# An attention with two gated layers in one kernel: first chunk's output products planned among the attention's steps, output copies of the first group on ScalarE, a longer warm-up and a later load

## The chip, the cores and the metric

The kernel runs on one core of a Trainium2 chip. The metric is the time of one execution on the device, in microseconds (us); lower is better. The core's engines are TensorE (PE, with its weight loads PEld), VectorE (DVE), ScalarE (ACT), GpSimd (POOL) and SyncE (SP), which here only issues DMA transfers. Each engine works through its own instructions in the order in which they stand, and waits on semaphores for the others.

## The reference, cut to what matters

```python
batch, n_heads, seq, head_dim = (4, 8, 576, 64)            # attention
scores = scale * np.matmul(q, k.transpose(0, 1, 3, 2))
thresh = np.max(scores, axis=-1, keepdims=True) - tau
scores = np.where(scores >= thresh, scores, -1000000000.0)
attn = softmax(scores);  x = attn @ v                       # x: 2304 tokens x 512
rms = np.sqrt(np.mean(x * x, axis=-1, keepdims=True) + 1e-06)
xn = x / rms * rms_g                                        # layer 1, d_ff = 1536
silu = g * (1.0 / (1.0 + np.exp(-g)))                       # g = xn @ w_gate
x = silu * (xn @ w_val) @ w_out
h = x @ w_in;  out = (h * np.cos(h)) @ w_out2               # layer 2, d_ff = 2048
```

The inputs are float32, except that the five large weights come as 64-bit floats; the kernel turns them into float32 itself.

## The kernel before, in words

**Attention.** The 32 heads are worked in 16 pairs. For a pair the kernel loads q, k and v, and PE transposes k and q in three preparations: `psb` (three quarters of k and its rest), `psa` (q) and `psc` (the last of k and the rests); ScalarE copies each out of PSUM. The rows of a pair form five units. `s_mm` makes the scores of a unit (a score block, tile `s`, two PSUM banks for each of the two heads, single buffered), VectorE copies them out and takes the row maximum (`s_max`), ScalarE makes the exponentials (`e`, for the fifth unit `el`), VectorE masks them and sums rows (`s_mask`), PE transposes the result (`pst`; the parts left over go to a `psc` of their own), ScalarE copies it (`et`), and PE multiplies with v (`po`, twice a pair). ScalarE copies that to `t`, GpSimd divides by the row sums (`xb<-t,rb`), squares it (`sq<-xb`) and adds the squares of a batch (`sq<-sq`); PE sums them over the features (`pss`), and VectorE, GpSimd and a trip through DRAM make the RMS factors `rs`. The attention's output goes to DRAM as well, and comes back in six chunks of 384 tokens.

**Layer 1.** Each chunk is scaled (`scale_x`, GpSimd, tile `acc<-acc,rs`; for the early chunks `xe<-xe`) and split into a high and a low part (`xh` on ScalarE, `xl` on VectorE), since every product is made of three matmuls (`mm3`: high x high, low x high, high x low). Layer 1 runs in six groups of two blocks of 128 features. For every group, chunk and block (numbered by `seq`), `gv_mm` makes the gate and value products (`pgv`, 24 matmuls of 384 columns), then come silu (`hh`), the product, and the split into `hhi` and `hlo`, and `o1` makes the output products (`px`, 12 matmuls into four PSUM banks: one tagged `v`, three tagged `t`, the same banks that the attention uses for `po`, for the transposes and for `pss`). After the second block of a group the four banks are added to `acc[c]`; in the first group (g == 0) they are copied. In the loop `o1` runs one step behind `gv_mm`. The next groups' weights are loaded (`raw`), converted (`wtmp`, with a step on GpSimd) and split (`whi`, `wlo`) on the way.

**Layer 2** follows in the same manner; the change doesn't touch it.

**What sets the order.** The attention and the first four steps of layer 1 (`N_EARLY = 4`: 96 matmuls `pgv` for chunks 0 and 1, without their output products) are steps of a planner, class `Plan`. Each step has an engine, a duration and a place from the table `STEPS`. `order` takes again and again the step that can start first by its own reckoning, and among equals the one with the lowest place, where place = the kind's number in `STEPS` + 3500 for each unit. It knows buffers (`take` and `free`), a port that VectorE and GpSimd share (`LOCK`, `BEHIND`: some GpSimd steps are made to wait for a VectorE instruction), and the PE's cost of changing between kinds of blocks. What it decides is the order of the program; on the chip each engine waits for its data. Ahead of the plan stand by hand: the loads of the first pair, `warm(8)` (products of ones that only keep PE at work), the three preparations of pair 0, with `warm(2)` behind the first. The plan starts with the loads of pair 1. Behind the plan, the rest of layer 1 is a loop written out in code.

Of the kernel before, what the change touches and what calls it, by code (L numbers as in the profile page):

```python
# [9 lines left out]
F32 = mybir.dt.float32  # L10
# [4 lines left out]
ALU = mybir.AluOpType  # L15
# [13 lines left out]
    "none": ("", 0, 27559),  # L29
    "load_k": ("SP", 1700, -172962, 5000),  # L30
    "load_q": ("SP", 1700, -46102, 7000),
    "load_v": ("SP", 1700, -4761, 5000),
    "pb": ("PE", 440, -19143),
    "pa": ("PE", 440, -15661),
    "pc": ("PE", 330, -8379),
    "pb_a": ("ACT", 590, 81106),
    "pa_a": ("ACT", 690, -473960),
    "pc_a": ("ACT", 480, 49428),
    "s": ("PE", 960, -21325),
    "s4": ("PE", 490, 85459),  # L40
    "warm": ("PE", 640, 37404),
    "max": ("DVE", 833, -172383),
    "exp": ("ACT", 785, 72251),
    "th": ("POOL", 300, -18608),
    "mask": ("DVE", 890, -37373),
    "t": ("PE", 438, 31564),
    "raw": ("ACT", 595, -92045),
    "c0": ("PE", 220, -3639),
    "c1": ("PE", 440, -315186),
    "c_raw": ("ACT", 415, 218185),  # L50
    "radd": ("POOL", 250, 94231),
    "rinv": ("DVE", 430, -4519),
    "r_out": ("SP", 2100, -108544, 2500),
    "r_in": ("SP", 1700, -320774, 11000),
    "av0": ("PE", 2110, -371909),
    "av1": ("PE", 2660, -60188),
    "avo": ("ACT", 420, 4517),
    "div": ("POOL", 1410, 8372),
    "xout": ("SP", 500, -179658, 2500),
    "sq": ("POOL", 1145, 63241),  # L60
    "x_add": ("POOL", 1410, 86580),
    "xsum": ("PE", 1150, 399585),
    "mean": ("DVE", 150, -681609),
    "rms": ("POOL", 1520, 138440),
    "rs_out": ("SP", 2500, -32428, 2500),
    "x_load": ("SP", 500, 48239, 6000),
    "x_p": ("POOL", 1010, 169405),
    "x_a": ("ACT", 610, -116593),
    "x_d": ("DVE", 550, 94630),
    "jdma": ("SP", 500, 52341, 5000),  # L70
    "j1": ("DVE", 600, -115045),
    "j2": ("DVE", 690, -98093),
    "j_p": ("POOL", 1310, 466908),
    "j_a": ("ACT", 620, 67088),
    "gv": ("PE", 2100, 18969),
    "silu": ("ACT", 500, -124840),
    "hmul": ("DVE", 560, -259566),
    "hhi": ("ACT", 520, -319947),
    "hlo": ("DVE", 560, -244125),
# [9 lines left out]
WARM = (8, 2, 0, 0)  # L89
# [7 lines left out]
N_EARLY = 4  # L97


class Plan:  # L100
# [19 lines left out]
    def order(self):  # L120
# [16 lines left out]
        while len(out) < len(steps):  # L137
            best = None
            for eng, ns in here.items():
                for n in list(ns):  # L140
                    s = steps[n]
                    held = [taken[tag][-self.bufs[tag]] for tag, _ in s["take"]
                            if len(taken[tag]) >= self.bufs[tag]]
# [46 lines left out]
    def run(self, tc):  # L190


        done = tc.nc.cur_bb.bb.instructions
        wait = mybir.DependencyInfo(mybir.DependencyClass.Sync, mybir.DependencyReason.DATA)
        for s in self.order():
            n = len(done)
            s["fn"]()
            if s["eng"] == "DVE" and s["kind"] in LOCK:
                s["ins"] = done[-1]
            if s.get("behind"):  # L200
                for x in done[n:]:
                    tc.add_manual_dep(x, s["behind"]["ins"].name, wait, reason="port")
# [3 lines left out]
def attention_moe_cos_kernel(  # L206
# [585 lines left out]

    def attention():
# [179 lines left out]
        def grow_2():  # L973
            att_s.close()
            late[2] = ctx.enter_context(tc.tile_pool(name="xhl2", bufs=1, side="right"))
            late["acc", 3] = ctx.enter_context(tc.tile_pool(name="acc3", bufs=1, side="right"))
# [25 lines left out]
        for n in range(N_EARLY):  # L1002
# [8 lines left out]
            hs.append(add("hlo", NU + n, h_lo, n, after=[x], free=[("hh", n)]))  # L1011
        plan.run(tc)

    with tc.manual_schedule():
# [11 lines left out]
        acc_p = ctx.enter_context(tc.tile_pool(name="acc", bufs=NCH - 1))  # L1026
# [3 lines left out]
        late.update({("acc", c): acc_p for c in range(NCH) if c != 3})  # L1030
# [7 lines left out]


        xacc = {}  # L1040

        def o1(n):
            g, c, i = seq[n]
            fs = groups[g][1]
            if i == fs[0]:
                xacc[c] = [
                    (ps_t if d else ps_v).tile(
                        [P, 512], F32, tag="t" if d else "v", name=f"px{d}"
                    )[:, 0:TC]
                    for d in range(KD)  # L1050
                ]
            whi, wlo = slots["1", 2, i]
            h = hq.pop(n)
            for d in range(KD):
                mm3(xacc[c][d], (whi[:, d], wlo[:, d]), h, i == fs[0], i == fs[-1])
            if i == fs[-1]:
                if c not in acc:
                    acc[c] = acc_tile(c, [P, KD, TC])
                for d in range(KD):
                    dst = acc[c][:, d]  # L1060
# [4 lines left out]
                del xacc[c]  # L1065
# [194 lines left out]
```

## Time and profile before

| | before |
|---|---|
| median of 3 runs | 1190.27 us (1190.05 to 1190.27) |
| the profiled execution | 1190.16 us |
| its span, first to last instruction | 1188.4 us |
| PE busy | 1162.2 us, 98% of the span |
| VectorE busy | 798.9 us, 67% |
| ScalarE busy | 647.4 us, 54% |
| GpSimd busy | 313.8 us, 26% |
| chain of work that ended last | PE 91% of the span |

The profile is of one execution. Its page gives the busy time of each engine, the chain of work that ended last, and the costliest groups of instructions; the trace behind it can be asked for stretches of time, for waits and for single instructions. A PE that is busy is not always PE at its peak: matmuls are pipelined, two are under way at a time, and the granted clock can fall to half. So for PE the distance between the starts of two instructions says more than the duration of one.

### The profile page before, as it was taken

What the parts mean: (1) busy time and instruction counts of PE and PEld (TensorE: products, weight loads), DVE (VectorE), ACT (ScalarE), POOL (GpSimd) and SP (SyncE); (2) the same over time, 40 slices, a digit from 0 to 9 for tenths busy, and PEclk for the clock granted to TensorE, in tenths of its full rate; (3) what the DMA queues carried; (4) which work ended last, traced back from release to release, by engine and by line L of the source; (5) the groups of instructions that cost most, each with busy time, mean ns of one, the idle gap of its engine ahead of it and who ended that gap; (6) DMA issues with size and microseconds to landing.
All of it is one profiled execution on the core that took longest, in us unless ns stands there. A gap on an engine that the chain in (4) does not pass through costs nothing.

```text
span 1188.4 us, 18206 instructions
## 1 busy us (share of the span) xinstructions
PE 1162.2 (98%) x6832; PEld 1021.9 (86%) x6832; DVE 798.9 (67%) x1571; ACT 647.4 (54%) x1210; POOL 313.8 (26%) x299
## 2 busy tenths in 40 slices
PE   8999999999989999999999999999999999999997
PEld 6666666666779999999999999999999999999996
DVE  5787787877547572642735538579688696876765
ACT  5887877777424231321312214377676676766663
POOL 1223435423543120110201102014334243332222
PEclk9999999999989999999999999999999999999999
DMA  5434424112352130110300202102112021000014
GB/s 130 111 95 126 105 75 131 51 41 71 121 165 72 54 107 1 46 61 1 91 17 23 85 1 59 49 1 71 36 37 71 1 71 36 18 19 1 1 53 107
DMA packets 99448, 71.66 MB, mean 60 GB/s; under 512 B 65040, under 2 KB 89360, under 8 KB 99360
## 3 DMA queue, kind: packets, MB, share of 16 engines
q1 hardware_dynamic: 98256, 70.20, 21.0%
q8 instruction: 54, 0.88, 0.3%
q10 hardware_dynamic: 1040, 0.26, 0.1%
q14 instruction: 34, 0.28, 0.1%
q0 software_dynamic: 64, 0.03, 0.0%
HBM read 60.95 MB, written 9.52 MB: 59 GB/s over the span
## 4 chain that ended last, share of the span: by engine, by line
PE 91%; issue 3%; DVE 2%; ACT 1%; POOL 1%; DMA 1%; SPq 0%; POOLq 0%; DVEq 0%; ACTq 0%
PE pgv L736 23%; PE ph L736 16%; PE po L736 16%; PE px L736 11%; PE s L504 8%; PE po L630 7%; PE pst L593 5%; PE psc L612 1%; PE psa L438 1%; PE warm L702 0%; PE psb L438 0%; DMA raw<-in_moe_w_out_dram 0%; DVE wtmp L308 0%; DVE hlo L772 0%; ACT et L603 0%
## 5 line engine op out<-in xcount | busy, mean ns | idle before, releaser
L736 PE MATMUL pgv<-xl,whi 128*128 128x384 f32 x576 | 193.9, 337 | 0.0
L736 PE MATMUL pgv<-xh,whi 128*128 128x384 f32 x576 | 193.9, 337 | 0.0
L736 PE MATMUL pgv<-xh,wlo 128*128 128x384 f32 x576 | 193.7, 336 | 0.0
L312 POOL TENSOR_TENSOR wtmp<-wtmp,raw 128x512 int32<-128x512 int32 x68 | 93.5, 1375 | 364.4 <-DVE wtmp L308 347.7
L1165 POOL TENSOR_TENSOR hlo<-r,hhi 128x384 fp32r<-128x384 f32 x96 | 98.0, 1021 | 303.7 <-ACT hhi L1164 247.7
L760 ACT ACTIVATE hh<-pgv 128x384 f32<-128x384 f32 x72 | 35.4, 491 | 255.9 <-PE pgv L736 255.9
L764 DVE TENSOR_TENSOR hh<-hh,pgv 128x384 f32<-128x384 f32 x72 | 39.8, 552 | 167.0 <-ACT hh L760 166.9
L736 PE MATMUL ph<-xh,whi 128*128 128x384 f32 x384 | 129.7, 338 | 0.0
L736 PE MATMUL ph<-xl,whi 128*128 128x384 f32 x384 | 129.6, 338 | 0.0
L736 PE MATMUL ph<-xh,wlo 128*128 128x384 f32 x384 | 129.3, 337 | 0.0
L524 DVE TENSOR_SCALAR_CACHE_REDUCE s<-s 128x576 f32<-128x576 f32 x128 | 91.9, 754 | 47.3 <-PE s L504 47.1
L1147 ACT ACTIVATE t<-ph,magic 128x384 f32<-128x384 f32 x96 | 55.8, 581 | 111.4 <-PE ph L736 111.4
L736 PE MATMUL po<-whi,hlo 128*128 128x512 f32 x288 | 114.7, 398 | 1.4 <-POOL hlo L1165 1.4
L736 PE MATMUL po<-whi,hhi 128*128 128x512 f32 x288 | 113.9, 395 | 0.2 <-ACT hhi L1164 0.2
L736 PE MATMUL po<-wlo,hhi 128*128 128x512 f32 x288 | 113.5, 394 | 0.0
L736 PEld LDWEIGHTS pgv<-xl,whi 128*128 128x128 f32 x576 | 108.2, 188 | 0.4 <-DVE xl L730 0.3
L736 PEld LDWEIGHTS pgv<-xh,whi 128*128 128x128 f32 x576 | 108.3, 188 | 0.0
L736 PEld LDWEIGHTS pgv<-xh,wlo 128*128 128x128 f32 x576 | 108.2, 188 | 0.0
L553 DVE SCALAR_TENSOR_TENSOR e<-s,th,e 128x576 f32<-128x576 f32 x128 | 103.1, 840 | 0.5 <-POOL th L534 0.5
L736 PE MATMUL px<-hhi,whi 128*128 128x384 f32 x288 | 98.9, 343 | 3.6 <-DVE acc L1062 3.3
L1154 DVE SCALAR_TENSOR_TENSOR r<-t,r 128x384 f32<-128x384 f32 x96 | 99.4, 1035 | 3.3
L543 ACT ACTIVATE e<-s,m 128x576 f32<-128x576 f32 x128 | 95.7, 783 | 8.2 <-DVE s L524 7.9
(118 smaller groups left out, 2457.6 us busy)
## 6 DMA issues: line engine op xcount, KB each, us to landing
raw<-in_moe_w_out_dram SPq DMA_DIRECT2D x28, 512.0 KB
raw<-in_moe_w_in_dram SPq DMA_DIRECT2D x16, 512.0 KB
raw<-in_moe_w_gate_dram SPq DMA_DIRECT2D x12, 512.0 KB
raw<-in_moe_w_val_dram SPq DMA_DIRECT2D x12, 512.0 KB
x<-xb SPq DMA_DIRECT2D x16, 288.0 KB
kn<-in_k_dram SPq DMA_DIRECT2D x16, 256.0 KB
vn<-in_v_dram SPq DMA_DIRECT2D x16, 256.0 KB
qn<-in_q_dram SPq DMA_DIRECT2D x15, 256.0 KB
```

Of the source, the lines that this page charges most:

```text
L312: nc.gpsimd.tensor_tensor(tmp, tmp, lw, op=ALU.add)
L504: nc.tensor.matmul(ps[:, c, 0:288], lhs, kh[r, k0:k0 + 288], start=True, stop=True,)
L524: nc.vector.tensor_scalar(s.rearrange("p (c n) -> p c n", c=2), un[n].pop(("ps", hd))[:, :, 0:288], qscale[:, 0:1] if n % 5 == 4 else 1.0, ...
L543: nc.scalar.activation(un[n]["e"][:, hd], un[n]["s", hd], AF.Exp, bias=grp[group_of(n)]["m"][:, c], scale=-1.0)
L553: nc.vector.scalar_tensor_tensor(e, un[n].pop(("s", hd)), grp[group_of(n)]["th"][:, ci:ci + 1], e, op0=ALU.is_le, op1=ALU.mult, accum_out= ...
L593: nc.tensor.transpose(ps[:, c], e[:, hd, k0:k0 + P], ident)
L630: nc.tensor.matmul(po[64 * hd:64 * hd + 64, :], vn[:, c, hd, :] if c < 4 else vl[:, hd, :], hf[j]["et"][:, hd, c, :] if c < 4 else hf[j][" ...
L736: nc.tensor.matmul(ps, w[a], x[bb], start=first and i == 0, stop=last and i == 2)
L764: nc.vector.tensor_tensor(hq[n], hq[n], pgv.pop(n)[:, 1, 0:TC], op=ALU.mult)
L1147: nc.scalar.activation(t, ph, AF.Identity, bias=magic[:, 0:1], scale=INV2PI)
L1154: nc.vector.scalar_tensor_tensor(r, t, -C2, r, op0=ALU.mult, op1=ALU.add)
L1165: nc.gpsimd.tensor_tensor(lo, r, f(hi), op=ALU.subtract)
```

## The change

Five things are changed. The warm-up ahead of the keys has 12 products instead of 8, and the 2 behind the first preparation are gone. The load of the second pair's keys waits for the last transpose of the first preparation (`load_k1`, a dependency added by hand). Two steps of output products (`px`, `N_PX = 2`, both blocks of chunk 0, 24 matmuls) and their four copies (`pxc`) are made steps of the plan, so the loop behind it starts with two of them done. The first group's copies of output products go from VectorE to ScalarE. And all numbers of the table `STEPS` that set the places are others, so that the planner's order changes everywhere. Chunk 0's sum moves to the pool of chunk 3's. The rest of the diff moves `o1` to another place in the file and counts two takes of one tag in a step properly.

```diff
 STEPS = {
...
-    "max": ("DVE", 833, -172383),
-    "exp": ("ACT", 785, 72251),
+    "max": ("DVE", 833, -2165065),
+    "exp": ("ACT", 785, 18525),
...
+    "px": ("PE", 2100, 184028),
+    "pxc": ("ACT", 500, 1363803),
...
-WARM = (8, 2, 0, 0)
+WARM = (12, 0, 0, 0)
...
+N_PX = 2
...
+    def px_out(g, c, d):
+        dst = acc[c][:, d]
+        if g == 0:
+            nc.scalar.copy(dst, xacc[c][d])
+        else:
+            nc.vector.tensor_tensor(dst, dst, xacc[c][d], op=ALU.add)
...
         for kind, m in zip("bac", WARM[1:]):
             prep_pe(0, kind)
+            if kind == "b":
+                first = tc.nc.cur_bb.bb.instructions[-1]
             prep_act(0, kind)
             warm(m)
+        def load_k1(p):
+            done_ = tc.nc.cur_bb.bb.instructions
+            n = len(done_)
+            load_k(p)
+            for x in done_[n:]:
+                tc.add_manual_dep(x, first.name, SYNC, reason="first loads")
...
-                lk[p] = add("load_k", n, load_k, p, take=[("kn", ("kn", p))])
+                lk[p] = add("load_k", n, load_k if p > 1 else load_k1, p, take=[("kn", ("kn", p))])
...
+        y = add("none", 999, lambda: acc.__setitem__(0, acc_tile(0, [P, KD, TC])), after=[g2])
+        z = None
+        for n in range(N_PX):
+            z = add("px", NU + n + 3, px_mm, n, after=[hs[n], z],
+                take=[] if n else [("v", ("px", 0))] + [("t", ("px", d)) for d in range(1, KD)],
+            )
+        for d in range(KD):
+            add("pxc", NU + 5, px_out, 0, 0, d, after=[z, y], free=[("v" if not d else "t", ("px", d))] if 0 else [("px", d)])
...
-                    if g == 0:
-                        nc.vector.tensor_copy(dst, xacc[c][d])
-                    else:
-                        nc.vector.tensor_tensor(dst, dst, xacc[c][d], op=ALU.add)
...
-        done = 0
+        done = N_PX
```

PE, early in the attention, where the second pair's scores meet the first's last transposes (`s_500` and `s_529` are the scores of two units, `el` the fifth unit's, `psa` the queries' preparation). Before:

```order
L617 MATMUL psc<-ident,el 64x128
L593 MATMUL pst<-ident,e 128x128 x8
L504 MATMUL s_500<-k,q 128x288
L504 MATMUL s_501<-k,q 128x288
...
L504 MATMUL s_529<-k,q 128x288
L504 MATMUL s_530<-k,q 128x288
...
L438 MATMUL psa<-ident,qn 128x128 x4
```

Now, at the same unit:

```order
L449 MATMUL psb<-ident,k_424 128x128
L444 MATMUL psb<-ident,kn 128x128 x3
L510 MATMUL s_531<-k,q 128x288
L510 MATMUL s_532<-k,q 128x288
...
L636 MATMUL po<-et,vn 64x320 x8
L636 MATMUL po<-ec,v_95 64x320 x2
L510 MATMUL s_568<-k,q 128x288
L510 MATMUL s_569<-k,q 128x288
```

The two score blocks that stood one behind the other have the first pair's second value products between them.

PE, at the end of the attention: the fifth unit's transposes of the last pair, its second value products `po`, the early gate and value products `pgv` (96), the last batch's row sums `pss` and the first output products `px`. Before:

```order
L593 MATMUL pst<-ident,el 128x128 x4
L736 MATMUL pgv<-xh,whi 128x384
...
L736 MATMUL pgv<-xh,wlo 128x384
L630 MATMUL po<-et,vn 64x320 x8
L630 MATMUL po<-ec,v_96 64x320 x2
L670 MATMUL pss<-ones,sq 128x1 x5
L736 MATMUL px_4139<-hhi,whi 128x384
```

Now:

```order
L599 MATMUL pst<-ident,el 128x128 x4
L636 MATMUL po<-et,vn 64x320 x8
L636 MATMUL po<-ec,v_96 64x320 x2
L742 MATMUL pgv<-xh,whi 128x384
...
L742 MATMUL px_4078<-hhi,wlo 128x384
L676 MATMUL pss<-ones,sq 128x1 x5
L742 MATMUL px_4174<-hhi,whi 128x384
```

The last value products have moved ahead of the 96, and the 24 output products of chunk 0 stand between the 96 and the row sums.

GpSimd, from the scaling of chunk 2 on (`xe`): the last batch's power (`r_149`), the scaling of chunks 3, 4 and 5 (`acc<-acc,rs`) and the weights' additions (`wtmp`). Before:

```order
L723 TENSOR_TENSOR xe<-xe 128x384 x2
L681 TENSOR_TENSOR r_149<-r_149,expo 128x5
L789 TENSOR_TENSOR acc<-acc,rs 128x1536
L312 TENSOR_TENSOR wtmp<-wtmp,raw 128x512 x3
L789 TENSOR_TENSOR acc<-acc,rs 128x1536
L312 TENSOR_TENSOR wtmp<-wtmp,raw 128x512 x2
```

Now:

```order
L729 TENSOR_TENSOR xe<-xe 128x384 x4
L795 TENSOR_TENSOR acc<-acc,rs 128x1536
L687 TENSOR_TENSOR r_149<-r_149,expo 128x5
L318 TENSOR_TENSOR wtmp<-wtmp,raw 128x512
L795 TENSOR_TENSOR acc<-acc,rs 128x1536
L318 TENSOR_TENSOR wtmp<-wtmp,raw 128x512 x2
```

The power and the scaling of chunk 3 have changed places, and one weight addition instead of three stands ahead of the scaling of chunk 4.

## Rows read from the trace of the kernel before

**Rows 1.** Stretch, its length; busy us of PE, PEld, DVE, ACT, POOL; clock; DMA, GB/s

```profile
10.00:305.00 295.00, 288.35 (x2163) 193.88 (x2164) 234.19 (x634) 226.78 (x412) 100.07 (x114) 1.00 0.36 94
...
328.00:335.00 7.00, 5.21 (x20) 5.21 (x21) 1.43 (x4) 1.23 (x2) 6.20 (x6) 0.51 0.07 25
335.00:400.00 65.00, 61.38 (x347) 59.76 (x346) 43.49 (x73) 22.82 (x44) 22.09 (x12) 1.00 0.42 128
400.00:1100.00 700.00, 699.58 (x3766) 668.29 (x3765) 449.02 (x734) 334.21 (x638) 147.39 (x127) 1.00 0.13 38
```

**Rows 2.** What PE waited for: us in total, times, longest

```profile
PE s L504 <- DVE s L524: 5.2, 7, 0.9
PE pss L670 <- POOL sq L661: 4.9, 1, 4.9
PE px L736 <- DVE acc L1062: 3.3, 3, 1.7
PE psb L443 <- DMA k<-in_k_dram: 2.4, 1, 2.4
...
PE pst L593 <- ACT et L603: 0.7, 1, 0.7
```

**Rows 3.** Instructions in order of time, start: start us, us, operation, [idle before]

```profile
7.34 1.06 PE L702 MATMUL warm<-ones 128*128 128x128 f32 x4
7.59 0.58 ACT L472 COPY k<-psb 128x512 f32<-128x512 f32 x1 [4.83 <-PE psb L438]
...
8.20 1.06 PE L438 MATMUL psa<-ident,qn 128*128 128x128 f32 x4
...
9.30 0.69 ACT L470 ACTIVATE q<-psa,qscale 128x512 f32<-128x512 f32 x1 [1.12 <-PE psa L438]
```

**Rows 4.** The same view of PE, second of two score blocks in a row

```profile
35.76 1.43 PE L504 MATMUL s<-k,q 64*128 64x288 f32 x6 [0.85 <-DVE s L524]
```

**Rows 5.** The same view: earlier row sums, then the attention's end on four engines

```profile
144.50 1.17 PE L670 MATMUL pss<-ones,sq 128*128 128x1 f32 x10
...
301.55 1.70 DVE L553 SCALAR_TENSOR_TENSOR el<-s,th,el 128x576 f32<-128x576 f32 x1 [0.21 <-POOL th L534]
...
305.00 0.42 PE L736 MATMUL pgv<-xh,whi 128*128 128x384 f32 x1
305.28 0.59 ACT L603 COPY et<-pst 128x512 f32<-128x512 f32 x1
...
325.44 1.40 POOL L647 TENSOR_TENSOR xb<-t,rb 128x576 f32<-128x576 f32 x1 [1.83 <-ACT t L640]
...
329.79 2.29 PE L670 MATMUL pss<-ones,sq 128*128 128x1 f32 x10 [4.89 <-POOL sq L661]
331.94 0.67 PE L736 MATMUL px<-hhi,whi 128*128 128x384 f32 x1
...
335.52 0.34 PE L736 MATMUL pgv<-xh,whi 128*128 128x384 f32 x1
...
339.68 0.34 PE L736 MATMUL px<-hhi,whi 128*128 128x384 f32 x1
```

**Rows 6.** PE's waits for the copies, and two groups of copies (count, busy, mean ns)

```profile
342.68 0.44 PE L736 MATMUL px<-hhi,whi 128*128 128x384 f32 x1 [0.75 <-DVE acc L1062]
...
353.00 0.41 PE L736 MATMUL px<-hhi,whi 128*128 128x384 f32 x1 [1.73 <-DVE acc L1062]
...
L1062 DVE COPY acc<-px 128x384 f32<-128x384 f32 x24 | 11.7, 547 | 0.0
...
L472 ACT COPY k<-psc 128x384 f32<-128x384 f32 x16 | 7.6, 474 | 0.9 <-PE psc L458 0.9
```

**Rows 7.** GpSimd's scaling of chunk 4, and PE's first products of chunk 4

```profile
356.56 3.50 POOL L789 TENSOR_TENSOR acc<-acc,rs 128x1536 f32<-128x1536 f32 x1
...
367.73 0.34 PE L736 MATMUL pgv<-xh,whi 128*128 128x384 f32 x1
```

More of the change, by code (lines that the diff above doesn't have):

```diff
@@ L28 @@
 STEPS = {
[L29 to L41, printed above, removed]
-    "max": ("DVE", 833, -172383),
-    "exp": ("ACT", 785, 72251),
@@ L44 @@
[L44 to L79, printed above, removed]
+    "none": ("", 0, 989236),
+    "load_k": ("SP", 1700, -2080791, 5000),
+    "load_q": ("SP", 1700, -71929, 7000),
+    "load_v": ("SP", 1700, 1092105, 5000),
+    "pb": ("PE", 440, -510840),
+    "pa": ("PE", 440, -238233),
+    "pc": ("PE", 330, 5527),
@@ new lines @@
+    "pb_a": ("ACT", 590, -16795),
+    "pa_a": ("ACT", 690, -1741191),
+    "pc_a": ("ACT", 480, -1089184),
+    "s": ("PE", 960, -2067487),
+    "s4": ("PE", 490, -536410),
+    "warm": ("PE", 640, -512436),
+    "max": ("DVE", 833, -2165065),
+    "exp": ("ACT", 785, 18525),
+    "th": ("POOL", 300, -79889),
+    "mask": ("DVE", 890, -806542),
+    "t": ("PE", 438, 45402),
+    "raw": ("ACT", 595, -536576),
+    "c0": ("PE", 220, -1677441),
+    "c1": ("PE", 440, -448255),
+    "c_raw": ("ACT", 415, -134803),
@@ L80 @@
+    "hmul": ("DVE", 560, 68682),
+    "hhi": ("ACT", 520, -551420),
+    "hlo": ("DVE", 560, -825852),
 }
@@ L141, in order @@
                     s = steps[n]
-                    held = [taken[tag][-self.bufs[tag]] for tag, _ in s["take"]
-                            if len(taken[tag]) >= self.bufs[tag]]
+                    tags = [tag for tag, _ in s["take"]]
+                    at = [(tag, len(taken[tag]) + tags[:i].count(tag) - self.bufs[tag]) for i, tag in enumerate(tags)]
+                    held = [taken[tag][i] for tag, i in at if i >= 0]
                     wait = [key for key in held if users.get(key, 1)]
@@ L201, in run @@
                 for x in done[n:]:
-                    tc.add_manual_dep(x, s["behind"]["ins"].name, wait, reason="port")
+                    tc.add_manual_dep(x, s["behind"]["ins"].name, SYNC, reason="port")
 @with_exitstack
@@ L791, in scale_x, with px_open, px_mm, o1 @@
         )
+    xacc = {}
+    def px_open(c):
+        xacc[c] = [
+            (ps_t if d else ps_v).tile([P, 512], F32, tag="t" if d else "v", name=f"px{d}")[:, 0:TC]
+            for d in range(KD)
+        ]
+    def px_mm(n):
+        g, c, i = seq[n]
+        fs = groups[g][1]
+        if i == fs[0]:
+            px_open(c)
+        whi, wlo = slots["1", 2, i]
+        h = hq.pop(n)
+        for d in range(KD):
+            mm3(xacc[c][d], (whi[:, d], wlo[:, d]), h, i == fs[0], i == fs[-1])
+    def px_out(g, c, d):
[4 more added lines that the diff above has]
+            nc.vector.tensor_tensor(dst, dst, xacc[c][d], op=ALU.add)
+    def o1(n):
+        g, c, i = seq[n]
+        px_mm(n)
+        if i == groups[g][1][-1]:
+            if c not in acc:
+                acc[c] = acc_tile(c, [P, KD, TC])
+            for d in range(KD):
+                px_out(g, c, d)
+            del xacc[c]
     def attention():
@@ L1029, in attention_moe_cos_kernel @@
         late.update({c: x_p for c in range(3, NCH)})
-        late.update({("acc", c): acc_p for c in range(NCH) if c != 3})
+        late.update({("acc", c): acc_p for c in range(NCH) if c not in (0, 3)})
         late.update({("rs", c): t_rs for c in range(4, NCH)})
```

57 lines of the change are left out of this document (33 added, 24 removed).

## The prediction, as it stood before the change was run

> **What bounds the kernel now.** I read first the busy time of the engines by stretch of the span [rows 1]. TensorE (PE) is busy 699.58 of the 700 us from 400 to 1100, all at a granted clock of 1.00, so nothing that the change does there can show. What can show lies ahead of it: the first 10 us; the attention from 10 to 305 us, where PE is idle 295 - 288.35 = 6.65 us; the attention's end, with the 7 us from 328 to 335 us that ran at a clock of 0.51, the lower of its two levels (1.2 of 2.4 GHz); and the 65 us after, idle 3.6 us. The list of what PE waited for [rows 2] names the causes: 5.2 us for VectorE's row maxima (s), 4.9 us for GpSimd's last sum of squares (pss), 3.3 us for VectorE's copies of the first group's output products (px), 2.4 us for the first keys (psb). The other engines have room: over the attention VectorE is busy 234 and ScalarE 227 of 295 us [rows 1]. So I take the kernel as a chain of PE work with holes, and ask of each edit which hole it closes and which it opens.
>
> **Start: longer warm-up, no warm products between the preparations, second keys later.** Before, two warm products (four halves) stood between the keys' transposes (psb) and the queries' (psa), from 7.34 us; psa started at 8.20, ScalarE copied the keys until 7.59 + 0.58 = 8.17 and the queries from 9.30 to 9.99, after which the first scores began [rows 3]. Without them psa starts where they stood. At the slow rate that they showed (1.06 us for four halves) psa ends at 8.40, the queries' copy of 0.69 at 9.14: a gain of 0.85. At full rate psa ends before the keys' copy does, and the queries' copy follows that: 8.17 + 0.69 = 8.9, a gain of 1.1. I take **1.0**. The additional products of the first warm-up lie in the wait for the keys and cost nothing. Holding the second pair's keys behind the first transposes holds SP's queue: behind it stand the third pair's keys, which waited for a buffer anyway, and the next loads, none of which PE waited for. What it gives lies between 0 and the 2.4 us that PE waited for the first keys [rows 2]; I take 0, because the first pair's loads were issued ahead of them on the same queue. Ends for this part: 0 and 3.5.
>
> The Trainium skill (TensorE: Matmul & The Clock Gate, Part 1) says that the clock gate's window runs freely against the kernel and that the number of slow matmuls at the start differs from run to run; by it the term would be 0.85 in one run and 1.1 in another. No row here shows two starts. The Trainium skill (DMA: Bandwidth & Descriptors, Queues, rings and completion order) says that a DMA engine takes turns between the queues that have work for it; by it the later keys could speed only the queries' loads, which ScalarE and GpSimd issue, and the sum would stay as it is.
>
> **The attention's order.** The table of numbers changes every place in the plan, so the whole attention stands in a new order; the work on PE is the same. Before, two score blocks followed each other directly at five places (first excerpt of the order). The second block needs the PSUM banks that VectorE is still reading: at the first such place PE stood 0.85 us inside the second block [rows 4]. Five times about 0.9 us makes 4.5 of the 5.2 us [rows 2]. In the new order no two blocks touch: the least between them is four transposes at one place, three warm products at two, eight transposes at four. I keep 0.9 us for those and for four more changes between kinds of blocks (178 in the order against 174), and take **3.6** as the gain. The upper end is all idle time of the stretch, 6.65 us [rows 1]. The trace can't show waits that only the new order makes; as the lower end of the forecast I let them eat the gain, 0.
>
> **The end of the attention.** Before, the last pair's value products (po) stood behind the 96 early gate and value products. Their copy, the division (from 325.44), the square and the sum on GpSimd all came after those, and PE stood 4.89 us before the last row sums (pss) at 329.79 [rows 5]. That pause also cost clock: in 328 to 335 us it was 0.51 [rows 1], the ten sums took 2.29 us where ten others took 1.17, and the twelve products behind them 335.52 - 331.94 = 3.58 where 24 of the same shape took 339.68 - 335.52 = 4.16, so 2.08 for twelve [rows 5]. Together 4.89 + 1.12 + 1.50 = 7.5 us. In the new order (second excerpt) the last value products stand before the 96; GpSimd then has the 17 us of those and the 4.2 us of chunk 0's output products for a chain that took 329.79 - 325.44 = 4.4 us, and PE reaches pss without a pause. The moved output products (24 matmuls) bring nothing of their own: they cost 4.16 us here as there, and without them the 17 us would still cover the chain. What is late next: the value products now wait for ScalarE's copy of the last transposes, until 305.28 + 0.59 where the 96 had started at 305.00 [rows 5], with the hand-over 1.0 us; and PE comes to the last masks with less work in hand, for which I take 0.9 us, between 0 and the 2 us of one mask beside GpSimd's work (1.70 us [rows 5]) and its hand-over. Net **5.6**, ends 4.5 and 6.5.
>
> **First group's output copies on ScalarE.** Four copies of 547 ns on VectorE per chunk become four on ScalarE, near the 474 ns that its copy of the same 128x384 takes [rows 6]: some 11 us over six chunks, where ScalarE is busy 23 of 65 us [rows 1]. Behind them on ScalarE stand the next chunk's split and the weights' casts; those are needed a round or two later, so I cost them at nothing; if that cover is gone, a chunk's four copies (1.9 us) are what it costs. PE's waits for these copies came where one chunk's output products followed the last chunk's directly, 0.75 and 1.73 us [rows 6]; the third is the rest of the 3.3, 0.8 us. With two products done in advance a group of gate and value products (4.16 us) stands between them, so the first two go whatever engine copies; of the third I take a part: **2.8**, ends 1.5 and 3.3.
>
> **The sum.** 1.0 + 3.6 + 5.6 + 2.8 = 13.0 us. The profiled execution took 1190.16 us (span 1188.4 and 1.8 around it), 0.1 under the median of the runs; 1190.16 - 13.0 = **1177.2 us**. With the upper ends, but 1.5 at the start, 1.5 + 6.65 + 6.5 + 3.3 = 18.0: 1172.2. With the lower ends 0 + 0 + 4.5 + 1.5 = 6.0: 1184.2.
>
> **Rivals.** A: the new order of the attention makes waits of its own, twice as long as those it removes, -5.2 instead of 3.6: 1177.2 + 8.8 = 1186.0. For it: every engine's queue is new and each runs in its order. Against: in the new order, as before, several other blocks stand between a score block and its own transposes.
>
> B: chunk 4's inputs come late. They need the last row sums, a trip through DRAM, a scaling on GpSimd and a split; before, PE reached chunk 4 at 367.73, 35.8 us behind pss's end at 331.94 [rows 5, 7], now after twelve output products and four rounds of 6.24 us, 2.1 + 25.0 = 27.1 us. Before, the scaling started at 356.56 and took 3.50, so it ended 28.1 us behind pss [rows 7]; if it did so again, with 0.6 each for the two halves of the split, PE would wait 2.2 us, and at most 35.8 - 27.1 = 8.7 if the whole chain took all the time that it had: 1179.4 to 1185.9. Against: GpSimd then did three weight additions first and now one (third excerpt).
>
> C, slower: ScalarE becomes a convoy. Its copies of the transposes stand behind exponentials that wait for VectorE, and PE has three banks for transposes; a wait that cost 0.7 us once [rows 2] would come in each of the 16 pairs. The other terms give 9.4, so it is slower by over 0.2% from (9.4 + 2.4)/16 = 0.74 us a pair; at 1.0 us a pair the time is 1190.16 - 9.4 + 16 = 1196.8. Nothing in the old trace shows ScalarE so late.
>
> D, the change doesn't do what it says: GpSimd's chain is held by the masks as before and pss waits all the same, the copies only move to another engine, and the attention gains nothing: 1190.16 - 1.0 = 1189.2.
>
> **Chances.** The forecast (1172.2 to 1184.2) 0.72, A 0.13, B 0.07, C 0.05, D 0.03. A measurement of this kernel can tell about 0.2%, 2.4 us, from no change. Faster by over that: 0.72 + 0.07 + 0.09 of A = 0.88; within it 0.03 of A and D = 0.06; slower C and 0.01 of A = 0.06. Range 1172.0 to 1186.0, which leaves out C, D and about half of A.
>
> **What would show it.** Right: no PE wait for the sum of squares, and a clock of 1.00 from 300 to 340 us; under 1 us of waits for row maxima; no wait for the copies of px above 1 us; first scores near 9 us; chunk 4's first products without a wait. Wrong: PE idle in the attention above 6.65 us, with waits of transposes for ScalarE (A, C); a wait of chunk 4's first products for their split (B); pss still waiting for GpSimd (D).

## The result, and the profile of the changed kernel

The changed kernel takes 1178.12 us (median of 4 runs, 1177.18 to 1178.91), the kernel before 1190.27: a ratio of 0.9895, with a 95% interval from 0.9878 to 0.9912. The forecast was 1177.2 in a range of 1172 to 1186, faster with a chance of 0.88. The total came out 0.9 us above the forecast, but two of its four terms were too small and two too large, and the largest miss is a wait that the forecast had given 7 chances in 100.

The profiled execution of the changed kernel took 1178.78 us; its span is 1176.8, against 1188.4 before: 11.6 us less. First the busy time of the engines by stretch (its start and length; busy us of PE, PEld, DVE, ACT, POOL; clock; DMA share, GB/s), with stretches moved by the shorter span so that they answer to [rows 1]:

```profile
320.00:327.00 7.00, 7.00 (x46) 7.00 (x45) 2.85 (x6) 4.51 (x10) 5.56 (x6) 1.00 0.17 63
327.00:392.00 65.00, 62.72 (x349) 61.80 (x349) 43.74 (x57) 31.09 (x66) 23.90 (x13) 0.97 0.40 128
392.00:1088.00 696.00, 695.59 (x3743) 664.31 (x3743) 445.49 (x728) 333.32 (x636) 147.54 (x127) 1.00 0.13 39
```

The 7 us at the attention's end, which ran at a clock of 0.51 before, are now fully busy at 1.00. The 65 us behind them have a clock of 0.97, where it was 1.00. The rest of the kernel is as full as it was. What PE waited for (us in total, times, longest), to be laid beside [rows 2]:

```profile
PE pgv L742 <- DVE xl L736: 2.3, 2, 1.8
...
PE po L636 <- ACT et L609: 1.3, 4, 0.7
...
PE s L510 <- DVE s L530: 0.3, 1, 0.3
```

The 4.9 us for the last sum of squares and the 3.3 us for the copies of px are gone from the list, and the waits for row maxima fell from 5.2 to 0.3. At its head stands a wait that wasn't in [rows 2]: gate and value products (pgv) of layer 1 wait 2.3 us for the low halves of their inputs (xl), which VectorE makes.

**Where the 11.6 us are.** But for the warm-up PE's work is the same in both kernels, so its path can be cut at the same pieces of work: the first scores, the first gate and value product, and the first such product of chunk 2 (335.52 us before, 328.37 after).

```profile
8.39 1.24 PE L510 MATMUL s<-k,q 64*128 64x288 f32 x8 [0.50 <-ACT q L476]
...
301.17 2.37 PE L636 MATMUL po<-et,vn 128*64 128x320 f32 x16 [0.68 <-ACT et L609]
...
304.01 0.44 PE L742 MATMUL pgv<-xh,whi 128*128 128x384 f32 x1
...
325.17 1.17 PE L676 MATMUL pss<-ones,sq 128*128 128x1 f32 x10
...
328.37 0.34 PE L742 MATMUL pgv<-xh,whi 128*128 128x384 f32 x1
```

These rows of PE in order of time (start us, us, operation) give:

| piece | before | after | gain |
|---|---|---|---|
| to the first scores | 10.04 | 8.39 | 1.65 |
| first scores to first gate product | 294.96 | 295.62 with 20 value products (304.01 - 301.17 = 2.84) more: 292.78 | 2.18 |
| from there to chunk 2 | 30.52 with the 20 value products and 12 output products; less 2.84, and with 24 more output products (4.16 [rows 5]): 31.84 | 24.36, with 36 output products | 7.48 |
| all that follows | the rest of 1188.4 | the rest of 1176.8 | 11.6 - 11.31 = 0.3 |

So the whole gain is made by 328 us, and the last row, in which the copies of px were to give 2.8 us, gave 0.3.

### The profile page after: what moved, and what is told of

The parts are those of the page before. It is cut to its first block, busy times and chain, and to the rows that moved or that the text cites. A ratio compares the mean times of both kernels' runs of the same rounds, so it can differ in the third digit from the quotient of the medians.

```text
span 1176.8 us, 18220 instructions
## 1 busy us (share of the span) xinstructions
PE 1162.3 (99%) x6836; PEld 1021.4 (87%) x6836; DVE 791.6 (67%) x1547; ACT 656.8 (56%) x1234; POOL 315.5 (27%) x299
## 4 chain that ended last, share of the span: by engine, by line
PE 92%; issue 3%; ACT 2%; DVE 2%; DMA 0%; POOL 0%; SPq 0%; POOLq 0%; ACTq 0%
PE pgv L742 24%; PE ph L742 16%; PE po L742 16%; PE px L742 12%; PE s L510 8%; PE po L636 7%; PE pst L599 5%; ACT et L609 1%; PE psc L618 1%; PE psa L444 1%; ACT e L549 0%; PE psb L444 0%; PE pss L676 0%; PE warm L708 0%; DVE xl L736 0%
```

## Experiments

Each edit below is against the changed kernel. They ask two things: what the new wait at pgv is, and what each part of the change is worth by itself.

### The new wait: who holds chunk 4's low halves?

The wait of 1.76 us is at 356.43, at the second product of chunk 4, the first that takes a low half. What VectorE and GpSimd did ahead of it in the changed kernel (start us, us):

```profile
344.63 3.73 DVE L309 TENSOR_SCALAR wtmp<-raw 128x512 int32<-128x512 int32 x1
...
351.86 3.98 DVE L328 TENSOR_TENSOR wlo<-wtmp,whi 128x512 fp32r<-128x512 f32 x1
355.77 2.19 DVE L736 SCALAR_TENSOR_TENSOR xl<-acc,g_sb,xh 128x384 fp32r<-128x384 f32 x4
```

```profile
344.12 3.96 POOL L795 TENSOR_TENSOR acc<-acc,rs 128x1536 f32<-128x1536 f32 x1
...
351.47 3.82 POOL L795 TENSOR_TENSOR acc<-acc,rs 128x1536 f32<-128x1536 f32 x1
```

The integer operation of L309, 0.42 us elsewhere, took 3.73, and the subtraction of L328, 0.68 elsewhere, 3.98: each began inside one of GpSimd's scalings (chunk 4's at 344.12, chunk 5's at 351.47) and ended 0.3 to 0.6 us behind it. Before the change the same scaling of chunk 4, from 356.56 to 360.06 [rows 7], fell into a pause of VectorE:

```profile
360.10 0.55 DVE L764 TENSOR_TENSOR hh<-hh,pgv 128x384 f32<-128x384 f32 x1 [4.65 <-ACT hh L760]
```

So theory P: while GpSimd scales, such instructions of VectorE on SBUF tiles stand still, and by that chunk 4 is late. The Trainium skill (SBUF — State Buffer, Who interferes with whom) has this as a rule: one pair of ports is shared by VectorE and GpSimd and is held for a whole instruction; a VectorE operation with two inputs in SBUF, or in a two-port mode, waits it out. The trace agrees with it for the subtraction, which has two inputs in SBUF, at 3.98 us; that the operation of L309, with one input, ran in such a mode no run here shows. Rival S: ScalarE made chunk 4's high halves only at 353.53, behind four copies of px (1.6 us). Rival L: the data came late through DRAM, as rival B of the prediction had it.

**e1: chunks 4 and 5 scaled on VectorE.**

```diff
-        nc.gpsimd.tensor_tensor(
+        eng = nc.gpsimd if c == 3 else nc.vector
+        eng.tensor_tensor(
             acc[c], acc[c], xrs[c][:, None, :].broadcast_to([P, KD, TC]), op=ALU.mult
         )
```

> The changed kernel, with one edit: the scalings of chunks 4 and 5 (128x1536, two of them) run on VectorE instead of GpSimd. Theory P (while GpSimd scales, VectorE's instructions with two inputs in SBUF stand still; that delayed chunk 4's split, so PE waited 1.76 us at its first product and then ran some 3.4 us at the lower clock): the wait falls under 0.5 us, the clock stays at 1.00 behind it, VectorE's subtraction and tensor_scalar that took 3.98 and 3.73 us take about 0.7 and 0.4, and the time falls by 1.3 + 1.6 = 2.9, to about 1175.2 us. Rival S (the split was late because ScalarE's four copies of chunk 2's output products, 1.6 us, stand ahead of it): the wait stays between 1.5 and 2 us and the time between 1177 and 1179. Rival L (the chunk's data come late through DRAM): VectorE now waits for them itself, the wait stays or grows, 1178 to 1181.

Measured: 1175.14 us (1174.82 to 1175.31), ratio to the kernel before 0.9872 (0.9855 to 0.9888). VectorE's rows of the same place, PE's wait for xl in all, and PE alone in the stretch that ran at 0.97 (start, length; busy us; clock; DMA share, GB/s):

```profile
344.79 0.42 DVE L309 TENSOR_SCALAR wtmp<-raw 128x512 int32<-128x512 int32 x1
345.12 2.86 DVE L796 TENSOR_TENSOR acc<-acc,rs 128x1536 f32<-128x1536 f32 x1
...
350.37 0.68 DVE L328 TENSOR_TENSOR wlo<-wtmp,whi 128x512 fp32r<-128x512 f32 x1
352.70 2.21 DVE L736 SCALAR_TENSOR_TENSOR xl<-acc,g_sb,xh 128x384 fp32r<-128x384 f32 x4 [1.65 <-ACT xh L732]
```

```profile
PE pgv L742 <- DVE xl L736: 0.5, 1, 0.5
```

```profile
335.00:400.00 65.00, 65.00 (x374) 1.00 0.41 128
```

L309 and L328 are back at 0.42 and 0.68, the low halves start at 352.70 in place of 355.77, the wait of 1.76 is gone, and PE is busy all of 335 to 400 us at a clock of 1.00. ScalarE's copies still stand ahead of the split (VectorE even waits 1.65 us for the first high half), and the data still come through DRAM, so S and L fall. The gain of the copies was there, and this collision had eaten it. VectorE does the scaling itself in 2.86 us (1.75 for chunk 5), GpSimd took 3.96 and 3.82.

**e8: the scalings in four pieces.** Same engine, same work, four instructions of 128x384 for each chunk.

```diff
-        nc.gpsimd.tensor_tensor(
-            acc[c], acc[c], xrs[c][:, None, :].broadcast_to([P, KD, TC]), op=ALU.mult
-        )
+        for kk in range(KD):
+            nc.gpsimd.tensor_tensor(acc[c][:, kk], acc[c][:, kk], xrs[c], op=ALU.mult)
```

> The changed kernel, with each of GpSimd's scalings of chunks 3, 4 and 5 (128x1536) cut into four of 128x384; same work, same engine. Theory P (VectorE stands still for one whole GpSimd instruction, and gets its turn between two): no VectorE instruction stands longer than about 1.2 us beside a scaling (before: 4.29 for two, 3.73 and 3.98), the waits of 1.76 and 0.52 us at the first products of chunks 4 and 2 fall under 0.3, and the time is 1174.7 to 1176. Rival (GpSimd's four pieces follow each other and VectorE gets no turn in between, or it is GpSimd's load and not the length of one instruction that counts): VectorE's long instructions stay at 3 to 4 us, 1177.2 to 1179.

Measured: 1177.70 us (1177.14 to 1178.98). Half of theory P's expectation came, and not its gain, and the time is in the rival's range. VectorE's rows, then GpSimd's of chunk 5:

```profile
347.89 1.50 DVE L328 TENSOR_TENSOR wlo<-wtmp,whi 128x512 fp32r<-128x512 f32 x1
352.78 5.26 DVE L736 SCALAR_TENSOR_TENSOR xl<-acc,g_sb,xh 128x384 fp32r<-128x384 f32 x4 [3.39 <-issue]
```

```profile
352.74 4.88 POOL L796 TENSOR_TENSOR acc<-acc,rs 128x384 f32<-128x384 f32 x4
```

VectorE does get its turn between two pieces: no single instruction stands for 3 us any more, and PE's wait of 0.52 at chunk 2 is gone. But chunk 4's four low halves now meet chunk 5's four pieces and take turns with them, 5.26 us in place of the 2.21 in e1, and PE waits 1.8 us over four places. In this profiled execution (1178.98 us) the clock was 0.71 from 357.0 to 360.4 us, behind waits of at most 0.50. So a shorter instruction of the other engine isn't enough here, as long as the two share the stretch just ahead of PE.

**e9: all three scalings on VectorE.** Chunk 3's too, which is a step of the plan.

```diff
-        nc.gpsimd.tensor_tensor(
+        nc.vector.tensor_tensor(
...
-        add("x_p", NU + 6, scale_x, 3, after=[x])
+        add("x_d", NU + 6, scale_x, 3, after=[x])
```

> The changed kernel with all three scalings (chunks 3, 4 and 5) on VectorE; in the plan chunk 3's stands ahead of chunk 2's last three low halves. Theory P (a GpSimd scaling holds up VectorE's two-input instructions for its length): besides the wait at chunk 4 also the 0.52 us at chunk 2's products goes, because the two low halves that took 4.29 us take about 1.15; 1175.1 - 0.5 = 1174.6, between 1174.2 and 1175.0. Rival (VectorE now waits for chunk 3's data, which land only about when it comes there, and chunk 0's gated products behind it are late): a wait of 0.5 to 2 us at chunk 0's output products or at pss, 1175.3 to 1177.

Measured: 1179.22 us (1176.61 to 1180.47). Theory P's half came true, PE waits for no low half at chunks 2 and 4 any more. So did the rival's wait at pss, 2.5 us, and the time is 2.2 above the rival's range. The plan put the scaling where the data had not landed. VectorE stood 2.90 us for them, and GpSimd, which the plan holds behind that step, stood 3.23 (rows of VectorE, GpSimd and ScalarE in order of time, and PE's wait):

```profile
322.09 1.76 DVE L795 TENSOR_TENSOR acc<-acc,rs 128x1536 f32<-128x1536 f32 x1 [2.90 <-DMA acc<-x]
```

```profile
323.98 2.32 POOL L729 TENSOR_TENSOR xe<-xe 128x384 f32<-128x384 f32 x2 [3.23 <-DVE acc L795]
```

```profile
326.86 0.84 ACT L821 COPY acc<-px 128x384 f32<-128x384 f32 x2
```

```profile
PE pss L676 <- POOL xe L729: 2.5, 1, 2.5
```

The list names GpSimd, but its last sum of squares was done at 320.75. What pss, which started at 327.84, still needed was a PSUM bank: ScalarE's second copy of chunk 0's output products ended at 327.70. Those copies stood on ScalarE behind chunk 2's split, and the split waited for GpSimd's late scalings of chunk 2 (xe).

On a busy engine a step that waits for a transfer costs more than it does on an idle one.

### The clock behind the new wait

In the profile of the changed kernel the clock fell to its lower level (0.51 from 357.0 to 360.4 us) behind the wait of 1.76. The kernel was run once more beside e9 and e11.

> The changed kernel itself again, beside the two others on the same chip. Expected 1177.2 to 1178.9: where the clock falls behind the 1.76 us wait at chunk 4's products the time is near 1178.8, where it doesn't near 1177.3, and both come about as often.

Measured: 1177.97 us (1176.68 to 1178.82). The profiled execution of this run took 1177.29, with the same wait and no fall. PE at chunk 4, first in the first profile, then in the second:

```profile
356.43 0.44 PE L742 MATMUL pgv<-xl,whi 128*128 128x384 f32 x1 [1.76 <-DVE xl L736]
...
357.66 0.52 PE L742 MATMUL pgv<-xh,whi 128*128 128x384 f32 x1
```

```profile
356.47 0.44 PE L742 MATMUL pgv<-xl,whi 128*128 128x384 f32 x1 [1.78 <-DVE xl L736]
...
357.63 0.34 PE L742 MATMUL pgv<-xl,whi 128*128 128x384 f32 x1
```

The times of the changed kernel lie in two groups, near 1177.2 and near 1178.8, four executions of each in the two runs; for the six without a profile here the cause is inferred from the time. A wait of 1.8 us costs 1.8 us in one execution and some 1.5 more (1178.78 - 1177.29) in another. Against the first group e1 gains 2.1 us, against the second 3.7. The Trainium skill (TensorE: Matmul & The Clock Gate, Part 1) says that the gate's window runs freely against the kernel; these two traces of one kernel agree, and in e1, where the wait is gone, the four runs lie within 0.5 us.

### What the engine of the copies is worth

**e2: the copies on VectorE again.**

```diff
-            nc.scalar.copy(dst, xacc[c][d])
+            nc.vector.tensor_copy(dst, xacc[c][d])
```

> The changed kernel, with the first group's copies of the output products on VectorE again. Theory (what took away PE's waits for these copies is the group of gate and value products that now stands between two chunks' output products, whatever engine copies): no wait of a px product above 0.5 us; VectorE gets 1.95 us more in front of chunk 4's low halves, so PE's wait there grows from 1.76 to 2.5 to 3.7 and the time is 1179 to 1180.5. Rival S (ScalarE's copies in front of the split are what makes chunk 4 late): the wait of 1.76 goes, 1175 to 1176.5. Rival (the engine matters to the px waits): px waits of 1 to 3 us are back, 1179.5 to 1181.5 with the waits at px.

Measured: 1178.69 us (1177.78 to 1179.61), 0.6 above the changed kernel. That is less than theory P expected, and the wait at chunk 4 fell to 1.4 us where 2.5 to 3.7 were expected. What PE waited for:

```profile
PE pgv L742 <- DVE xl L736: 1.4, 1, 1.4
...
PE pss L676 <- DVE acc L821: 0.8, 1, 0.8
...
PE px L742 <- DVE acc L821: 0.2, 1, 0.2
```

The px waits of 0.75 and 1.73 [rows 6] stay away though VectorE copies, so the products in advance do away with them whatever engine copies, as the prediction had it. New is 0.8 us at pss, whose PSUM bank VectorE empties later. Why the wait at chunk 4 neither went nor grew, two rows of VectorE, then GpSimd and ScalarE:

```profile
352.13 1.94 DVE L821 COPY acc<-px 128x384 f32<-128x384 f32 x4
...
356.04 2.19 DVE L736 SCALAR_TENSOR_TENSOR xl<-acc,g_sb,xh 128x384 fp32r<-128x384 f32 x4
```

```profile
351.75 3.82 POOL L795 TENSOR_TENSOR acc<-acc,rs 128x1536 f32<-128x1536 f32 x1
```

```profile
352.31 2.13 ACT L732 ACTIVATE xh<-acc,g_sb 128x384 fp32r<-128x384 f32 x4
```

The copies, which read PSUM, took 1.94 us beside GpSimd's scaling, as long as four of them took with nothing beside them before the change (1.95). They filled time in which VectorE's subtraction would have stood still, so the low halves came only 0.3 us later than in the changed kernel. The high halves came 1.2 us sooner (353.53 there), and the low halves didn't follow: a second refutation of rival S.

**e11: e2 and e1 together**, so that the collision doesn't cover the difference.

> The changed kernel with the scalings of chunks 4 and 5 and the first group's copies of the output products on VectorE. It shows what ScalarE's copies are worth by themselves, without the collision. Theory (VectorE, with the copies, empties the banks of chunk 0's products later, so pss waits 0.8 us and one px product 0.25; chunk 4's low halves come 1.9 us later, just when PE wants them): 1175.1 + 0.8 + 0.3 = 1176.2, between 1175.7 and 1177. Prediction's reading (the engine that copies doesn't matter): 1174.8 to 1175.4.

Measured: 1176.32 us (1176.0 to 1177.67), against 1175.14 in e1. With the collision out of the way ScalarE's copies are worth 1.2 us, in two waits of PE (for the second 0.25 was expected):

```profile
PE pss L676 <- DVE acc L822: 0.8, 1, 0.8
PE px L742 <- DVE acc L822: 0.8, 1, 0.8
```

### What the products in advance are worth

**e3: no products in advance.**

```diff
-N_PX = 2
+N_PX = 0
...
-        for d in range(KD):
+        for d in range(KD if N_PX else 0):
```

> The changed kernel without products in advance: chunk 0's 24 output products and their copies stand in the loop behind the attention, as before the change, with copies on ScalarE and all other places in the order kept. Theory of the prediction (the products in advance bring nothing at the row sums, but they do away with the px waits): pss still doesn't wait for GpSimd's sums, since the 96 products cover 4.4 us of chain; px waits of 0.75 + 1.73 + 0.8 come back in about that size, so 1179.5 to 1181.5 if chunk 4's wait stays. Rival (the 4.2 us of products in advance are needed as cover): pss waits 1 to 4 us, and the time is 1181 to 1185. If chunk 4's wait of 1.76 us (with 1.6 of clock) goes at the same time because the row sums come 4.2 us sooner against PE's rounds, 3.3 less: 1176 to 1178.

Measured: 1182.51 us (1182.02 to 1182.81), 4.4 above the changed kernel and above the range of the prediction's theory. pss started at 320.92 without a wait, as expected. But the px waits came back at 0.57 in all, and the loss is elsewhere. PE's waits behind pss, and PE alone in the 7 us after them:

```profile
326.35 0.44 PE L742 MATMUL pgv<-xh,whi 128*128 128x384 f32 x1 [1.02 <-ACT xh L732]
...
327.07 0.44 PE L742 MATMUL pgv<-xl,whi 128*128 128x384 f32 x1 [0.28 <-DVE xl L736]
...
330.99 0.69 PE L742 MATMUL pgv<-xl,whi 128*128 128x384 f32 x1 [3.13 <-DVE xl L736]
```

```profile
330.00:337.00 7.00, 6.01 (x19) 0.51 0.70 218
```

Without the 24 products PE reaches chunk 2 about 4.2 us sooner, at 324.12, before its inputs are split, waits 1.02, 0.28 and 3.13 us there, and 330 to 337 us run at a clock of 0.51. The 3.13 is the same collision again: one low half of chunk 2 took 3.65 us beside GpSimd's scaling of chunk 3. So the products in advance have a use that the prediction did not see: they stand between the last row sums and chunk 2 and cover its inputs.

### Order of the attention, and its end

**e4: the old table of places.** All other edits are kept; `px` and `pxc` keep the change's numbers.

> The changed kernel with the table of places of the kernel before (and the two new steps with the change's numbers): the attention stands in its old order, the last value products behind the 96 gate and value products and now behind the 24 output products as well; warm-up, late keys, products in advance and ScalarE's copies are kept. Theory (the new order is what closes the five waits between score blocks and the wait at the last row sums): five waits of about 0.9 us for row maxima are back (2.2 us of time net), pss waits about 4.9 us for GpSimd and the clock falls behind it, 7.5 us; 1178.1 + 9.7 = 1187.8, between 1185.5 and 1189.5. Rival (the products in advance cover the wait at the row sums in any order): pss waits under 1 us, 1180 to 1182.

Measured: 1189.83 us (10 runs, 1187.28 to 1190.41), so 11.7 above the changed kernel, nearly all of its gain, and 0.3 above the expected range. The five waits for row maxima are back (`s`), and pss waits longer than in the kernel before. What PE waited for:

```profile
PE pss L676 <- POOL sq L667: 6.6, 1, 6.6
PE s L510 <- DVE s L530: 5.2, 7, 0.9
PE pgv L742 <- DVE xl L736: 1.8, 1, 1.8
```

The old places put the products in advance ahead of the last value products, where they delay GpSimd's chain along with PE; and chunk 3's scaling (3.75 us) now got onto GpSimd ahead of the last division. The rival, that the products in advance cover the row sums in any order, falls.

**e7: the old table, with the last value products ahead of the 96.**

```diff
+            last_av = x
             outs[j] = add("avo", n1, av_out, j, after=[x, outs[j - 1] if par else None], free=[("v", j)],
...
-            x = add("gv", NU + n, gv_mm, n, 0, after=(x0, x1)[c] + jops + [smm[NU - 1], g1],
+            x = add("gv", NU + n, gv_mm, n, 0, after=(x0, x1)[c] + jops + [smm[NU - 1], g1, last_av],
```

> The changed kernel with the table of places of the kernel before, but with the last value products ahead of the 96 gate and value products: of the new order only that one swap. Theory (two separate gains: the swap does away with the wait at the last row sums and the lower clock behind it; the five separated pairs of score blocks are worth about 2.2 us of time, not the 3.6 of the prediction): pss doesn't wait for GpSimd, s waits for the row maxima 5.2 us in all, and the time is 1178.1 + 2.2 = 1180.3, between 1179.5 and 1181. Rival (the score blocks are worth the predicted 3.6): 1181.7. Rival (the old order holds GpSimd's chain behind the masks all the same): pss waits 2 to 5 us, 1182 to 1187.

Measured: 1180.68 us (1180.48 to 1180.86). What PE waited for:

```profile
PE s L510 <- DVE s L530: 5.2, 7, 0.9
PE pgv L742 <- DVE xl L736: 2.9, 2, 1.5
```

pss doesn't wait; the swap of one pair of blocks is worth 1189.83 - 1180.68 = 9.2 us against e4. The rest of the new order is worth 1180.68 - 1178.12 = 2.6 us. The collision at the low halves is here too, 2.9 us against 2.3, without a fall of the clock in the profile, so the better measure of the attention is the traces up to the first gate product, with the first scores as origin: 306.85 - 8.41 - (304.01 - 8.39) = 2.8. So both gains are there and separate, and the score blocks' is nearer to 2.2 than to 3.6.

### The start

**e5: the old warm-up**, `WARM = (8, 2, 0, 0)`.

> The changed kernel with the old warm-up: eight products at first and two between the keys' and the queries' transposes. Theory W (the longer warm-up gives the whole gain at the start, because TensorE works until just before the keys come and the granted clock stays at 1.00; before, it was at the lower level from 7.3 to 10.7 us): the first scores start 1.0 to 1.7 us later than 8.39, near 9.4 to 10.0, the clock falls to the lower level for some 3.4 us after the wait for the keys, and the time is 1179.2 to 1180.1. Rival K (the later keys of pair 1 give it, by bringing the first keys sooner): the first scores within 0.4 us of 8.39 and the time within 0.5 of 1178.1.

Measured: 1181.19 us (1180.81 to 1181.60), 3.1 above the changed kernel and 1.1 above theory W's range; by the trace 1.7 of it at the start (the first scores at 10.10, not 8.39). The keys came as early as in the changed kernel (6.53 and 6.50), so the whole 1.7 is the warm-up's. PE in order of time:

```profile
6.53 0.45 PE L449 MATMUL psb<-ident,k 128*128 128x128 f32 x1 [1.72 <-DMA k<-in_k_dram]
...
7.41 1.06 PE L708 MATMUL warm<-ones 128*128 128x128 f32 x4
...
8.26 1.06 PE L444 MATMUL psa<-ident,qn 128*128 128x128 f32 x4
```

psa takes 1.06 us as in [rows 3]; in the changed kernel it took 0.60 (at 6.96). The longer warm-up does more than fill the wait: it keeps PE at its rate through it. For e5 that rests on the durations alone: the kernel before has a granted clock of 0.50 from 7.3 to 10.7 us, while e5's profile lists 1.00 there. Of the 3.1 us the two profiled executions, which both show the fall of the clock at chunk 4, leave 1180.82 - 1178.78 = 2.0; the 0.3 of these beyond the start, and why the medians lie further apart, are not explained.

**e6 and e12: the second pair's keys at once**, `load_k` for every pair, in the changed kernel and in e1.

> The changed kernel, with the second pair's keys loaded at once instead of behind the first transposes. Prediction's term (holding those keys back gives nothing, because the first pair's loads are ahead of them on the queue): the first keys' transposes start within 0.2 us of 6.50, the time within 0.4 of 1178.1. Rival K (the second pair's keys share the DMA engines with the first pair's): the transposes start 0.4 us later or more, near 6.9 as in the kernel before, and the time is 1178.4 to 1179.5.

> The changed kernel with the scalings of chunks 4 and 5 on VectorE (1175.14 us, its executions within 0.5 us of each other) and the second pair's keys loaded at once. Prediction's term (late keys give nothing): the first transposes start between 6.3 and 6.9 us and the time is 1174.8 to 1175.4. Rival K (the second pair's keys compete with the first pair's for the DMA engines): the transposes start near 7.2 us as in the other run with early keys, and the time is 0.5 to 0.8 longer, 1175.6 to 1176.0.

Measured: e6 1177.68 us (1177.37 to 1179.21), e12 1175.43 (1175.35 to 1175.51) against 1175.14 in e1. The first transposes, in e6 and in e12, started at 7.22 and 6.91:

```profile
7.22 0.30 PE L449 MATMUL psb<-ident,k 128*128 128x128 f32 x1 [0.70 <-DMA k<-in_k_dram]
```

```profile
6.91 0.30 PE L449 MATMUL psb<-ident,k 128*128 128x128 f32 x1 [1.00 <-DMA k<-in_k_dram]
```

In the eleven profiles with late keys, the changed kernel's among them, they started between 6.50 and 6.77; in the three with early keys, the kernel before among them, between 6.87 and 7.22. So rival K is right that the early keys hold up the first ones, by some 0.1 to 0.7 us. In the whole time it is 0.3 in e12, and e6 came out 0.4 below the changed kernel, inside the spread that the clock at chunk 4 makes: this edit's worth is at most a few tenths and is not told apart from nothing.

## Why the prediction was right, and where its steps failed

**Start: forecast 1.0, measured 1.65.** The mechanism stands and the size was low. The prediction had 8.9 us for the first scores "at full rate" and 9.14 at the slow one. PE did run at full rate (psa 0.60 us; e5 shows that the warm-up is the reason), and the keys came 0.37 us sooner, 6.50 against 6.87, a term that it had set to 0: 8.9 - 0.4 = 8.5, and 8.39 was measured. The reason for the 0, that the first pair's loads were issued ahead on the same queue, doesn't hold in e6 and e12.

**Order of the attention: forecast 3.6, measured 2.18, or 2.9 without the new wait for ScalarE's copy that the prediction had put into the next term.** The waits for row maxima went as forecast, 5.2 to 0.3, and PE's idle time between first scores and first gate product from 6.6 to 2.8. The step that failed is to count an idle hole as time gained, with no more than 0.9 us set against it:

```profile
10.04:305.00 294.96, 288.34 (x2163) 1.00 0.36 94
```

```profile
8.39:304.01 295.62, 292.81 (x2183) 1.00 0.37 96
```

(PE's busy time of the piece before and after; the columns are as in e1.) Idle time fell by 3.8 us, but busy time rose by 4.47 for 20 value products that took 2.84: 1.6 us came back inside the instructions. Where exactly, and why, is open; the new order has 178 changes between kinds of blocks against 174, and no run shows that these are the cause.

**End of the attention: forecast 7.5 less 1.0 and 0.9, measured 7.48 less 0.68.** The gross gain came as worked out, with the clock at 1.00 from 300 to 340 us, and pss without a wait. The wait for ScalarE's copy was 0.68 at 301.17, where 1.0 was taken; the 0.9 us for the last masks never came. That "the moved output products bring nothing of their own" was right at the row sums (e3: pss doesn't wait without them) and wrong behind them: e3 lost 4.4 us, at chunk 2.

**Copies of px on ScalarE: forecast 2.8, and 0.3 was left.** The px waits went, all 3.3 us of them, and for the reason given (e2). What failed is the sentence on what is late next. The prediction's rival B had the place, chunk 4's first products, and a wait of 2.2 us; 1.76 was measured, with 0.52 at chunk 2, and in the profiled execution 1.5 of clock, which the rival had not counted. But its reason was wrong: the chain through DRAM was done at 348.08, where chunk 4's scaling ended, 6 us before PE came. Late were VectorE's low halves, and they were late because two of GpSimd's scalings lay on VectorE's instructions (e1). The prediction had looked at the queues for order, and at what the engine beside it does at the same moment only for the masks; in [rows 7] the scaling was harmless only because VectorE paused for 4.65 us there.

The sum came this close by luck, because the errors cancel: +0.65 at the start, -1.4 at the order, +1.9 at the end, -2.5 at the copies: -1.4 against 13.0, so 11.6. (With the 0.68 us counted at the end of the attention, as the prediction did, the order missed by -0.7 and the end by +1.2.)

**The best version seen** is e1, 1175.14 us: the change, with chunks 4 and 5 scaled on VectorE.

## What to carry to other kernels

When a change moves work, ask of each long instruction on GpSimd which VectorE instructions it will now lie beside, not only in which order the queues stand: a scaling of 3.5 us cost nothing in a pause of VectorE, and two of 3.8 to 4.0 us cost some 3 us (e1) where they lay ahead of what TensorE wanted. The cheapest large gain here was to put a block whose result goes through a long chain ahead of work that needs nothing from it (9.2 us from one swap, e7 against e4), and a filler in that place is worth most where it also covers the next inputs (4.4 us). The length of an idle hole of TensorE isn't what closing it gives: 3.8 us of idle time closed in the attention gave 2.2 us, and the 4.9 us at the last row sums, with a clock of 0.51 behind them, gave 7.5.

## What the runs showed of the hardware

- VectorE's operation of L309 and its subtraction of L328, both on SBUF tiles, stood for as long as a GpSimd scaling ran beside them: 0.42 became 3.73 and 0.68 became 3.98 beside scalings of 3.96 and 3.82. Four copies out of PSUM kept their 1.94 us beside one of 3.82 (e2). Between four short GpSimd instructions VectorE gets its turn, but four low halves took 5.26 us in place of 2.21 (e8).
- The same wait of 1.76 us on TensorE was followed by 3.4 us at the lower clock in one execution and by full rate in another, 1.5 us apart. A longer warm-up across a wait of about 2 us for the first data kept the first transposes at full rate (0.60 us for four in place of 1.06).
- 128x1536 elements in float32 were scaled in 1.75 to 2.86 us on VectorE and in 3.4 to 4.0 on GpSimd.
- Loads that are issued behind others on the same queue slowed these: the first transposes of the keys started at 6.50 to 6.77 us without the second pair's behind them, at 6.87 to 7.22 with them.
